# Attention, two feed-forward layers, one core: a written order for the first 22 blocks

## The chip, the cores and the metric

The kernel runs on one core of a Trainium2 chip. The metric is the device time of one execution in microseconds, as the median of several executions. TensorE (PE) does the matmuls and loads their weights (PEld), VectorE (DVE), ScalarE (ACT) and GpSimd (POOL) do the elementwise work, and SyncE (SP) issues nearly all DMAs. Each engine carries out its own instructions strictly in the order in which they were written; an instruction whose input or buffer isn't ready holds up everything behind it on that engine.

## The reference, cut to what matters

```
a = exp(phi - max over sequence); a = a / (sum + 1e-9)      # phi: 8 x 8 x 576 x 32
k_m, v_m = a^T k, a^T v                                     # 32 memory rows per head
p = softmax(q k_m^T / 8);  attn = p v_m                     # q, k, v: 8 x 8 x 576 x 64
x = attn as 4608 x 512
h = x @ w_in;  g = h - tanh(h);  x = g @ w_out              # 512 -> 2048 -> 512
h = x @ w_in2; g = h if h > 0 else exp(h) - 1; out = g @ w_out2
```

The weights arrive as 64-bit floats and are turned into 32-bit ones on the chip.

## The kernel before, in words

**Attention units.** There are 16 units u0 to u15, one per batch and group of four heads. A unit is a Python generator (`Attention.unit`) that writes its instructions in some twenty steps: column maxima of phi (`cmax`, DVE), their transpose (`mT`, PE), the maximum (`nmax`, DVE), a diagonal (`dmax`), its broadcast (`bmax`, PE; copied by ACT into `bm`), `a = phi - bm`, the exponential (ACT), the memory matmuls (`km`, PE), normalisation (`rs`, `kvs`), transposes of q (`pq`, PE; `qT`, ACT) and of the memory (`kT_ps`), scores (`sc`, PE), a transpose into `s` (DVE), softmax on `s` (L237 to L245), a transpose into `phl`, a split into high and low part (ACT, then L255), and a store to DRAM.

**Conversions.** A generator `conv` loads 512 KB of raw weights, takes the magnitude on ACT into the one PSUM buffer `cv_m` (L55), works on it in two pairs of DVE instructions (L57 and L58, L61 and L64) and, for w_out, splits it (ACT L69, POOL L71). There are three raw buffers. Twelve conversions have to be over before block 2.

**First layer.** A half-block is one quarter of the columns of w_in for 288 tokens: `h_unit` (12 matmuls of 128x288 per row below, L374), then the activation on `h_ps` in pieces: ACT `t` (tanh, L385), `u` (L386), `s` (L387) and `big` (L396); POOL `v` (L392); DVE L401, L406 and L410; then the split `g` (ACT L416, POOL L417). Two x units (12 matmuls each, `x_ps`, L432) multiply the g of earlier half-blocks by w_out. `vw_unit` (L356, L360, L361) multiplies the attention's v_m into w_in; a half-block can't begin before its vw is there. I count half-blocks from 0; two make a block, and there are 64 blocks.

**What sets the order.** The string `PLAN` names for each half-block the pieces in their order: H the h unit, A the three ACT pieces, B, R, d, e, p the other pieces, G the split of the half-block before, X an x unit, V the vw unit. U or u moves every live attention unit on by one step, C or c the conversions. So units and conversions advance by rounds, all together. The PSUM pool `misc` has three banks, which bmax, km, pq, sc, vw_ps and x_ps share.

**Second layer.** `step2` writes for unit idx the h unit, the activation's first part (`e_a`), the split of the unit before (`e_c`: ACT L517, POOL L518), the activation's second part (`e_b`) and the output matmuls of unit idx-2 (L534). The last two units of all have nothing behind them. `store` puts each result of 128 rows into DRAM with two DMAs, all on SP's queue.

Of the kernel before, what the change touches and what calls it, by code (L numbers as in the profile page):

```python
# [26 lines left out]
TB = 256  # L27
# [8 lines left out]
PLAN = ((1, "WHCABLlXRUGVXdepcCcu"),  # L36
        (14, "WHABLlXRCUGVXdepcCcu"),
        (44, "lWHLABCXRUXGdeVucp", "WcHAlBUXLRCVGdecXup"),
        (64, "WHAVUBCRlGdULYXUUecp", "WLHuARlCBXVduueYGp"),
        (128, "WuHALRlBCuVXedGYcpU", "lWHuABXRUdCLuYVuUeGp", "WlHUABYRLCdueXucVGp", "UWHLAVRlCUdXBeXGp"))  # L40
# [6 lines left out]
def convert(nc, pool, psum, raw, dst, whole=False):  # L47
# [7 lines left out]
    nc.scalar.activation(m, w_hi.bitcast(F32), ACTF.Abs)  # L55
    yield
    nc.vector.tensor_scalar(m, m, hi_lim, lo_lim, op0=ALU.min, op1=ALU.max)  # L57
    nc.vector.tensor_scalar(mu, mu, 3, 0x3FFFFFFF, op0=ALU.logical_shift_left, op1=ALU.bitwise_and)  # L58
    yield
    a = pool.tile(list(w_hi.shape), F32, tag="a", name="cv_a")  # L60
# [19 lines left out]
class Attention:  # L80
# [46 lines left out]
    def unit(self, u, nxt, eng, first_p=None):  # L127

        nc, wk, sm = self.nc, self.wk, self.sm
        b, g = divmod(u, 2)  # L130
# [26 lines left out]
        (nc.vector if u < 6 else eng).tensor_scalar(dmax, ident, nmax, None, op0=ALU.mult)  # L157
# [10 lines left out]
        eng.tensor_tensor(av, ph, bm.rearrange("p h (o m) -> p h o m", o=1).to_broadcast([96, 4, 6, M]),  # L168
                          op=ALU.subtract)
        yield  # L170
        if eng is nc.gpsimd:
            yield
# [21 lines left out]
        nc.vector.tensor_scalar(kvs, twice, rs, None, op0=ALU.mult)  # L194
# [43 lines left out]
        nc.vector.tensor_tensor(s, s, smax.to_broadcast([128, 18, M]), op=ALU.subtract)  # L238
# [6 lines left out]
        eng.tensor_tensor(s, s, smax.to_broadcast([128, 18, M]), op=ALU.mult)  # L245
# [7 lines left out]
        for t, src in parts:  # L253
            nc.scalar.activation(t[:, 0], src, ACTF.Copy)
            eng.tensor_tensor(t[:, 1], src, r32(t[:, 0]), op=ALU.subtract)  # L255
# [12 lines left out]
def make_const(nc, const):  # L268
# [7 lines left out]
    return {"ident": ident, "ones": ones, "bias": bias}  # L276

# [42 lines left out]
class Moe1:  # L320


    def __init__(self, tc, ctx, const, p_dram, x2_dram):
# [8 lines left out]
        self.vw, self.p, self.g, self.x2, self.work, self.x2_pool = {}, {}, {}, {}, {}, {}  # L332
# [46 lines left out]
    def g_a(self, n, pg):  # L379

        nc, w, bias = self.nc, self.work[n, pg], self.const["bias"]
# [4 lines left out]
        nc.scalar.activation(u, w[0], ACTF.Square)  # L386
        nc.scalar.activation(s, u, ACTF.Square, bias=bias[:, 0:1], scale=G_S)  # L387
# [24 lines left out]
    def g_d(self, n, pg):  # L412
        nc = self.nc
        s = self.work.pop((n, pg))[3]
        g = self.g_p.tile([128, 2, 2, NB], F32R, tag="g", name="g")
        nc.scalar.activation(g[:, 0], s, ACTF.Copy)  # L416
        nc.gpsimd.tensor_tensor(g[:, 1], s, r32(g[:, 0]), op=ALU.subtract)  # L417
        self.g[n, pg] = g
# [31 lines left out]
class Moe2:  # L450
# [70 lines left out]
    def o_unit(self, u):  # L521
# [6 lines left out]
        for tg in range(n_t):  # L528
# [8 lines left out]
            if k == last:  # L537
# [5 lines left out]
                self.store(c * TB + 128 * tg, o)  # L543

    def store(self, t0, o):
        done = 0
        while done < 128:
# [5 lines left out]
            self.nc.sync.dma_start(out=rows[p:p + step], in_=o[done:done + step])  # L553
# [3 lines left out]
def moe_kernel(tc, q, k, v, phi, w1, w2, w3, w4, out):  # L557
    nc = tc.nc
    with ExitStack() as top, tc.manual_schedule():
# [26 lines left out]
        def need(kind, pg, with_units=False):  # L586
            while not all((1, kind, pg, c) in converted for c in range(2)):
                cv.round()
                if with_units:
                    units.round()  # L590

        def conv(layer, kind, pg, c, lead=2):
# [6 lines left out]
            else:  # L599
                r0 = 256 * pg + 128 * c  # L600
                nc.sync.dma_start(out=raw, in_=w[r0:r0 + 128, :])
            for k in range(lead + 1):
# [20 lines left out]
            yield from convert(nc, cv_p, cv_ps, raw, dst, whole)  # L623
# [16 lines left out]
        for what in "phi", "kv", "q0", "q1":  # L640
            at0.load(0, what)
            at1.load(1, what)
        at1.load(2, "phi")
# [287 lines left out]
```

## Time and profile before

| what | value |
|---|---|
| median of 3 runs | 1657.15 us (1656.73 to 1658.26) |
| the profiled execution | 1656.48 us, of which the span from first to last instruction is 1654.7 us |
| PE busy | 1580.8 us, 96% of the span |
| DVE, ACT, POOL busy | 1143.8, 906.7, 744.6 us |
| mean granted TensorE clock | 0.982 of full speed |
| first h unit begins | 63.20 us |

A row of a view names the start in us, the duration in us, the engine, the line and the instruction with the tile that it writes and those that it reads. The bracket at its end is the idle time of that engine just before, and what ended it.

### The profile page before, as it was taken

What the parts mean: (1) busy time and instruction counts of PE and PEld (TensorE: products, weight loads), DVE (VectorE), ACT (ScalarE), POOL (GpSimd) and SP (SyncE); (2) the same over time, 40 slices, a digit from 0 to 9 for tenths busy, and PEclk for the clock granted to TensorE, in tenths of its full rate; (3) what the DMA queues carried; (4) which work ended last, traced back from release to release, by engine and by line L of the source; (5) the groups of instructions that cost most, each with busy time, mean ns of one, the idle gap of its engine ahead of it and who ended that gap; (6) DMA issues with size and microseconds to landing.
All of it is one profiled execution on the core that took longest, in us unless ns stands there. A gap on an engine that the chain in (4) does not pass through costs nothing.

```text
span 1654.7 us, 28097 instructions
## 1 busy us (share of the span) xinstructions
PE 1580.8 (96%) x10742; PEld 1380.2 (83%) x10742; DVE 1143.8 (69%) x1664; ACT 906.7 (55%) x1639; POOL 744.6 (45%) x526
## 2 busy tenths in 40 slices
PE   5679989899999999999999999999999999999998
PEld 4558878788999999999999888888888888888886
DVE  5777768889998888887656655656565556555644
ACT  2356778678888888888753333333333333333332
POOL 0235667676765577777643332323222323232322
PEclk9779999999999999999999999999999999999999
DMA  9656677677754577675695211212121212121100
GB/s 238 184 170 185 188 210 217 197 226 237 249 182 153 180 222 223 220 223 179 204 336 217 91 64 39 89 39 89 39 77 40 75 39 76 41 74 52 38 1 26
DMA packets 142213, 232.89 MB, mean 141 GB/s; under 512 B 8704, under 2 KB 102912, under 8 KB 140032
## 3 DMA queue, kind: packets, MB, share of 16 engines
q1 hardware_dynamic: 142080, 231.11, 44.8%
q8 instruction: 84, 1.38, 0.3%
q14 instruction: 49, 0.40, 0.1%
HBM read 157.68 MB, written 73.40 MB: 140 GB/s over the span
## 4 chain that ended last, share of the span: by engine, by line
PE 81%; DVE 6%; ACT 4%; issue 4%; POOL 3%; DMA 1%; SPq 0%; POOLq 0%; ACTq 0%; DVEq 0%
PE h_ps L492 24%; PE o_ps L534 24%; PE x_ps L432 19%; PE h_ps L374 10%; PE vw_ps L356 2%; PE km L180 1%; DVE s L406 1%; POOL v L392 1%; DMA q<-in_q_dram 1%; POOL g L417 1%; ACT t L385 1%; ACT u L386 1%; DMA raw<-in_moe_w_in_dram 1%; DVE h_ps L401 0%; ACT x L438 0%
## 5 line engine op out<-in xcount | busy, mean ns | idle before, releaser
L518 POOL TENSOR_TENSOR e<-hm,e 128x512 fp32r<-128x512 f32 x144 | 186.6, 1296 | 573.7 <-ACT e L517 526.3
L432 PE MATMUL x_ps<-g,w 128*128 128x288 f32 x3072 | 437.5, 297 | 5.9 <-ACT x L438 2.2
L432 PEld LDWEIGHTS x_ps<-g,w 128*128 128x128 f32 x3072 | 417.4, 189 | 11.6 <-ACT x L438 3.1
L492 PE MATMUL h_ps<-x,wi 128*128 128x512 f32 (+1 forms) x1920 | 422.2, 370 | 0.0
L534 PE MATMUL o_ps<-wo,e 128*128 128x512 f32 x1728 | 420.4, 392 | 0.7 <-POOL e L518 0.7
L492 PEld LDWEIGHTS h_ps<-x,wi 128*128 128x128 f32 x1920 | 336.0, 188 | 65.7
L534 PEld LDWEIGHTS o_ps<-wo,e 128*128 128x128 f32 x1728 | 323.6, 188 | 72.4 <-POOL e L518 1.1
L503 ACT ACTIVATE t_ps<-hm 128x512 f32<-128x512 f32 x144 | 86.7, 602 | 501.5 <-DVE hm L502 501.5
L417 POOL TENSOR_TENSOR g<-s,g 128x576 fp32r<-128x576 f32 x128 | 198.2, 1549 | 115.4 <-ACT g L416 91.5
L392 POOL TENSOR_TENSOR v<-t,u 128x576 f32<-128x576 f32 x128 | 185.3, 1448 | 129.5 <-ACT u L386 105.8
L509 DVE SCALAR_TENSOR_TENSOR hm<-hm,t_ps 128x512 f32<-128x512 f32 x144 | 99.0, 687 | 200.3 <-ACT hm L504 200.3
L374 PE MATMUL h_ps<-p,vw 128*128 128x288 f32 x1536 | 235.5, 303 | 0.0
L374 PEld LDWEIGHTS h_ps<-p,vw 128*128 128x128 f32 x1536 | 214.4, 192 | 13.2 <-issue 11.7
L502 DVE TENSOR_SCALAR hm<-h_ps 128x512 f32<-128x512 f32 x144 | 99.5, 691 | 126.7 <-PE h_ps L492 124.0
L406 DVE SCALAR_TENSOR_TENSOR s<-s,v 128x576 f32<-128x576 f32 x128 | 137.2, 1072 | 54.3 <-ACT big L396 35.7
L385 ACT ACTIVATE t<-h_ps 128x576 f32<-128x576 f32 x128 | 83.4, 652 | 100.9 <-issue 42.6
L410 DVE COPY_PREDICATED s<-big,h_ps 128x576 f32<-128x576 uint32 x128 | 105.9, 828 | 7.9
L401 DVE TENSOR_TENSOR h_ps<-h_ps,t 128x576 f32<-128x576 f32 x128 | 97.1, 759 | 18.9 <-ACT u L386 18.5
L387 ACT ACTIVATE s<-u,bias 128x576 f32<-128x576 f32 x128 | 99.6, 778 | 16.3 <-POOL g L417 6.0
L510 DVE SCALAR_TENSOR_TENSOR hm<-hm,t_ps 128x512 f32<-128x512 f32 x144 | 98.9, 687 | 5.0
L511 DVE TENSOR_TENSOR hm<-hm,h_ps 128x512 f32<-128x512 f32 x144 | 98.9, 687 | 5.0
L504 ACT ACTIVATE hm<-hm 128x512 f32<-128x512 f32 x144 | 91.0, 632 | 13.1
(88 smaller groups left out, 1553.5 us busy)
## 6 DMA issues: line engine op xcount, KB each, us to landing
x_dram<-x SPq DMA_DIRECT2D x128, 288.0 KB, 3.4
xr<-x_dram SPq DMA_DIRECT2D x72, 512.0 KB, 3.8
p<-p_dram SPq DMA_DIRECT2D x62, 576.0 KB, 5.4
raw<-in_moe_w_in_dram SPq DMA_DIRECT2D x32, 512.0 KB, 4.5
raw<-in_moe_w_out_dram SPq DMA_DIRECT2D x32, 512.0 KB, 4.5
w_dram<-wst SPq DMA_DIRECT2D x32, 512.0 KB, 3.9
kv<-in_k_dram SPq DMA_DIRECT2D x16, 576.0 KB, 6.1
kv<-in_v_dram SPq DMA_DIRECT2D x16, 576.0 KB, 7.9
```

Source lines behind the costliest of these rows:

```text
L374: nc.tensor.matmul(ps[:, j, :NB], lhsT=vw[a][:, kc, c0 + 128 * j:c0 + 128 * j + 128], rhs=p[:, kc, b, :], start=(k == 0), stop=(k == 5))
L385: nc.scalar.activation(t, w[0], ACTF.Tanh)
L387: nc.scalar.activation(s, u, ACTF.Square, bias=bias[:, 0:1], scale=G_S)
L392: nc.gpsimd.tensor_tensor(v, t, u, op=ALU.mult)
L406: nc.vector.scalar_tensor_tensor(s, s, G_B, v, op0=ALU.add, op1=ALU.mult)
L410: self.nc.vector.copy_predicated(s, big.bitcast(U32), d)
L417: nc.gpsimd.tensor_tensor(g[:, 1], s, r32(g[:, 0]), op=ALU.subtract)
L432: nc.tensor.matmul(ps, lhsT=wo[pg][a][:, j, 128 * dm:128 * dm + 128], rhs=self.g[n, pg][:, b, j, :], start=(k == 0), stop=(k == 11))
L492: nc.tensor.matmul(out, lhsT=w3[:, a, kc, 128 * j:128 * j + 128], rhs=x[:, b, kc, :], start=(i == 0), stop=(i == 11))
L502: nc.vector.tensor_scalar(hm, w[0], 0.0, None, op0=ALU.min)
L518: nc.gpsimd.tensor_tensor(e[:, 1], hm, r32(e[:, 0]), op=ALU.subtract)
L534: nc.tensor.matmul(acc, lhsT=e[:, a, jj, 128 * tg:128 * tg + 128], rhs=w4[:, b, j, :], start=(k == 0 and jj == 0 and i == 0), stop=(k == l ...
```

## The change

The order of the first 22 blocks (44 half-blocks) is no longer made by rounds. `BEGIN` lists the steps before the first half-block, `SCRIPT` those of each of the first 44: u3 moves unit 3 on by one step, c6 conversion number 6, v writes a vw unit, p0 loads unit 0's phi. The three ACT pieces of A are now A, a and s, and the low part of the split (POOL) is g. From half-block 44 on the old plan goes on, with a, s and g right behind A and G.

`POOLS` says per unit which of the steps d (`dmax`), a, m (the softmax's product), l (the low part) run on POOL and whether k (`kvs`) runs on ACT; before, u0 and u1 had all on DVE, u2 to u5 a, m and l on POOL, and the others all four on POOL. In effect m of u3 and of u9 and l of u10 go from POOL to DVE, and `kvs` of u0 and u8 from DVE to ACT.

In the second layer the split of the last but one unit is written ahead of the last h unit, and half of the last eight stores go on ACT's queue.

```diff
-PLAN = ((1, "WHCABLlXRUGVXdepcCcu"),
...
+SCRIPT = ("W H c5 l c6 c6 A a R s B X u2 u3 u4 u4 G g V X d e L c6 c8 c7 u2 p c5 u3",
+          "W H c7 A a s L B l X R u2 c6 c6 u3 u4 G g X V d e p c7 c7 c9 c8 u2",
...
+POOLS = ("k", "", "aml", "al", "aml", "aml", "daml", "daml", "damlk", "dal", "dam", "daml", "daml", "daml", "daml", "daml")
+CLAMPS = ()
...
-        eng.tensor_tensor(s, s, smax.to_broadcast([128, 18, M]), op=ALU.mult)
+        on("m").tensor_tensor(s, s, smax.to_broadcast([128, 18, M]), op=ALU.mult)
...
+        if "k" in where:
+            nc.scalar.activation(kvs, twice, ACTF.Copy, scale=rs)
+        else:
+            nc.vector.tensor_scalar(kvs, twice, rs, None, op0=ALU.mult)
...
         def step2(idx):
+            if idx == len(seq) - 1:
+                m2.e_c(seq[idx - 1])
             if idx < len(seq):
                 m2.h_unit(seq[idx])
                 m2.e_a(seq[idx])
-            if 1 <= idx <= len(seq):
+            if 1 <= idx <= len(seq) and idx != len(seq) - 1:
                 m2.e_c(seq[idx - 1])
...
-                self.store(c * TB + 128 * tg, o)
-
-    def store(self, t0, o):
+                end = wide and c + 2 == NT // TB
+                self.store(c * TB + 128 * tg, o, (nc.scalar if tg % 2 == 0 else nc.sync) if end else nc.sync)
...
+    def step(self):
+        if not self.over:
+            try:
+                next(self)
+            except StopIteration:
+                pass
```

The first place is DVE shortly before the first half-block; `vw` is the split of the vw unit's result, `p` that of the first units' softmax, `cv_m` and `cv_a` belong to conversions. Before:

```order
L255 TENSOR_TENSOR p<-phl,p 128x288 x2
L57 TENSOR_SCALAR cv_m<-cv_m 128x512
L58 TENSOR_SCALAR cv_m<-cv_m 128x512
L61 SCALAR_TENSOR_TENSOR cv_m<-raw,cv_m 128x512
L64 SCALAR_TENSOR_TENSOR cv_a<-raw,cv_m 128x512
L361 TENSOR_TENSOR vw<-vw_ps,vw 128x256 x4
```

And now, from the same p on:

```order
L311 TENSOR_TENSOR p<-phl,p 128x288 x2
L439 TENSOR_TENSOR vw<-vw_ps,vw 128x256 x2
L107 TENSOR_SCALAR cv_m<-cv_m 128x512
L110 TENSOR_SCALAR cv_m<-cv_m 128x512
L113 SCALAR_TENSOR_TENSOR cv_m<-raw,cv_m 128x512
L116 SCALAR_TENSOR_TENSOR cv_a<-raw,cv_m 128x512
L439 TENSOR_TENSOR vw<-vw_ps,vw 128x256 x2
```

The first of the two vw splits has moved ahead of a whole conversion.

The second place is PE from half-block 1's h unit to half-block 2's; `sc` are unit u2's scores, `bmax` the broadcast of unit u3's or u4's maxima. Before:

```order
L374 MATMUL h_ps<-p,vw 128x288 x12
L77 MATMUL sc<-ident 128x128 x5
L230 MATMUL sc<-qT,kT 32x288 x8
L206 MATMUL pq<-ident,q 128x96 x3
L160 MATMUL bmax<-dmax,ones 96x128
L374 MATMUL h_ps<-p,vw 128x288 x12
```

And now:

```order
L452 MATMUL h_ps<-p,vw 128x288 x12
L129 MATMUL sc<-ident 128x128 x5
L286 MATMUL sc<-qT,kT 32x288 x8
L452 MATMUL h_ps<-p,vw 128x288 x12
L213 MATMUL bmax<-dmax,ones 96x128
L262 MATMUL pq<-ident,q 128x96 x6
```

The h unit has moved ahead of the bmax and of the transposes of q.

The third place is POOL in half-blocks 28 and 29; `w` is a conversion's split, `s` the softmax's product. Before:

```order
L392 TENSOR_TENSOR v<-t,u 128x576
L71 TENSOR_TENSOR w_3263<-cv_a,w_3262 128x512
L245 TENSOR_TENSOR s<-s,smax 128x576
L157 TENSOR_SCALAR dmax<-ident,nmax 128x128
L417 TENSOR_TENSOR g<-s,g 128x576
L392 TENSOR_TENSOR v<-t,u 128x576
L255 TENSOR_TENSOR phl<-phl 128x2x288
L168 TENSOR_TENSOR a<-phi,bm 96x4x6x32
```

And now:

```order
L476 TENSOR_TENSOR v<-t,u 128x576
L123 TENSOR_TENSOR w_3296<-cv_a,w_3295 128x512
L210 TENSOR_SCALAR dmax<-ident,nmax 128x128
L505 TENSOR_TENSOR g<-s,g 128x576
L476 TENSOR_TENSOR v<-t,u 128x576
L221 TENSOR_TENSOR a<-phi,bm 96x4x6x32
```

The product s has gone from in front of dmax, and the low part phl from in front of a.

## Rows read from the trace of the kernel before

**Rows 1.** Windows of the span: busy us (instructions) per engine, PE clock, DMA share.

```profile
0.00:64.00 64.00, 37.37 (x332) 28.11 (x333) 42.57 (x80) 18.29 (x43) 6.95 (x11) 0.84 0.91 232
64.00:116.00 52.00, 35.98 (x302) 27.09 (x300) 34.79 (x61) 25.81 (x53) 19.64 (x14) 0.71 0.56 160
116.00:437.00 321.00, 296.37 (x2903) 265.00 (x2903) 264.88 (x400) 241.63 (x476) 212.04 (x151) 0.99 0.69 207
437.00:841.00 404.00, 404.00 (x3481) 390.76 (x3480) 334.76 (x479) 338.12 (x591) 276.31 (x188) 1.00 0.63 205
```

**Rows 2.** Timeline of PE, 58 to 116 us: start, duration, instruction, idle before.

```profile
59.03 1.10 PE L356 MATMUL vw_ps<-w,vm 64*32 64x256 f32 x14 [7.21 <-DVE vw L361]
...
63.20 1.84 PE L374 MATMUL h_ps<-p,vw 128*128 128x288 f32 x12
...
80.72 0.74 PE L160 MATMUL bmax<-dmax,ones 128*96 128x128 f32 x2 [4.08 <-DVE s L234]
...
113.49 1.02 PE L356 MATMUL vw_ps<-w,vm 64*32 64x256 f32 x8 [3.33 <-DVE w L64]
```

**Rows 3.** Timeline of DVE, 54 to 112 us.

```profile
55.02 0.83 DVE L255 TENSOR_TENSOR p<-phl,p 128x288 fp32r<-128x288 f32 x2 [1.05 <-ACT p L254]
55.77 0.69 DVE L57 TENSOR_SCALAR cv_m<-cv_m 128x512 f32<-128x512 f32 x1
...
58.56 0.75 DVE L361 TENSOR_TENSOR vw<-vw_ps,vw 128x256 fp32r<-128x256 f32 x2
...
90.28 0.70 DVE L57 TENSOR_SCALAR cv_m<-cv_m 128x512 f32<-128x512 f32 x1 [5.11 <-ACT cv_m L55]
...
108.82 0.70 DVE L57 TENSOR_SCALAR cv_m<-cv_m 128x512 f32<-128x512 f32 x1 [1.04 <-ACT cv_m L55]
...
110.94 1.18 DVE L238 TENSOR_TENSOR s<-s,smax 128x576 f32<-128x576 f32 x1
```

**Rows 4.** Timeline of ACT, 84 to 90 us.

```profile
84.44 0.65 ACT L385 ACTIVATE t<-h_ps 128x576 f32<-128x576 f32 x1 [3.17 <-PE h_ps L374]
...
89.64 0.61 ACT L55 ACTIVATE cv_m<-raw 128x512 f32<-128x512 f32 x1
```

**Rows 5.** Timeline of PE, 209 to 327 us.

```profile
209.91 0.46 PE L160 MATMUL bmax<-dmax,ones 128*96 128x128 f32 x2 [1.36 <-POOL dmax L157]
...
232.19 0.46 PE L160 MATMUL bmax<-dmax,ones 128*96 128x128 f32 x2 [1.34 <-POOL dmax L157]
...
304.36 0.46 PE L160 MATMUL bmax<-dmax,ones 128*96 128x128 f32 x2 [3.40 <-POOL dmax L157]
304.58 3.07 PE L374 MATMUL h_ps<-p,vw 128*128 128x288 f32 x12
...
318.14 2.16 PE L180 MATMUL km<-kv,a 96*32 96x192 f32 x48 [1.38 <-ACT a L173]
...
326.08 1.16 PE L356 MATMUL vw_ps<-w,vm 64*32 64x256 f32 x32 [1.60 <-DVE kvs L194]
```

**Rows 6.** Timeline of POOL, 302 to 312 us.

```profile
302.07 1.16 POOL L245 TENSOR_TENSOR s<-s,smax 128x576 f32<-128x576 f32 x1 [0.41 <-DVE smax L244]
303.20 1.11 POOL L157 TENSOR_SCALAR dmax<-ident,nmax 128x128 f32<-128x128 f32 x1
...
310.45 1.43 POOL L255 TENSOR_TENSOR phl<-phl 128x576 fp32r<-128x576 f32 x1
```

**Rows 7.** Timeline of DVE, 315 to 326 us.

```profile
315.98 2.83 DVE L238 TENSOR_TENSOR s<-s,smax 128x576 f32<-128x576 f32 x1
...
323.13 0.73 DVE L242 TENSOR_REDUCE smax<-s 128x18 f32<-128x576 f32 x1
...
325.44 0.48 DVE L194 TENSOR_SCALAR kvs<-km,rs 128x256 f32<-128x256 f32 x1
```

**Rows 8.** Timeline of the end: PE's last matmuls.

```profile
1643.46 5.33 PE L534 MATMUL o_ps<-wo,e 128*128 128x512 f32 x22 [0.68 <-POOL e L518]
```

**Rows 9.** Timeline of the end: DVE's last copy.

```profile
1648.83 0.69 DVE L542 COPY o<-o_ps 128x512 f32<-128x512 f32 x1 [0.69 <-PE o_ps L534]
```

**Rows 10.** Timeline of the end: SP's DMA issues.

```profile
1647.38 4.06 SPq L553 DMA_DIRECT2D out_dram<-o  x8
```

More of the change, by code (lines that the diff above doesn't have):

```diff
@@ L584, in moe_kernel, with need, conv @@
         converted = set()
[L586 to L592, printed above, removed]
+        def need(kind, pg):
+            for c in range(2):
+                while (1, kind, pg, c) not in converted:
+                    if (kind, pg, c) in named:
+                        named[kind, pg, c].step()
+                    else:
+                        cv.round()
+        def conv(layer, kind, pg, c):
             w = {("i", 1): w1, ("o", 1): w2, ("i", 2): w3, ("o", 2): w4}[kind, layer]
@@ L657, in moe_kernel, with all_units @@
         first_p = [m1.new_p(0, n) for n in range(2)]
-        units = Staged()
-        for u in range(2 * B):
-            units.at((0, 1, 7, 13, 19, 25, 32, 39, 45, 52, 58, 65, 78, 85, 92, 99)[u], unit(u))
-        while 1 not in p_done:
-            if units.rounds >= 7:
-                cv.half()
-            units.round()
-            if units.rounds >= 7:
-                cv.round()
+        units = [Work(unit(u)) for u in range(2 * B)]
+        vw0 = []
+        def all_units():
+            live = [g for g in units if g.begun and not g.over] or [g for g in units if not g.begun][:1]
+            for g in live:
+                g.step()
@@ new lines, in first_vw, with side @@
+        def first_vw():
+            if not vw0:
+                m1.new_vw(0, 0, 0)
+            if len(vw0) < 2 and all((1, "i", len(vw0), c) in converted for c in range(2)) and vm_done >= {0, 1}:
+                m1.vw_unit(vm[:, 0], {len(vw0): wi[len(vw0)][0]}, 0, [len(vw0)])
+                vw0.append(True)
+        def side(step):
+            if step[0] == "u":
+                units[int(step[1:])].step()
+            elif step[0] == "c":
+                convs[int(step[1:])].step()
+            elif step == "v":
+                first_vw()
+            else:
+                u, what = int(step[-1]), {"p": "phi", "k": "kv", "q": "q0", "r": "q1"}[step[0]]
+                (at1 if u else at0).load(u, what)
@@ L667, in moe_kernel @@
+        for step in BEGIN.split():
+            side(step)
+        while 1 not in p_done:
+            all_units()
         pro.close()
@@ L824, in moe_kernel @@
                 pg = 2 * sw + i
[L825 to L826 removed]
+                hb = 2 * bi + i
+                for step in SCRIPT[hb].split() if hb < len(SCRIPT) else next(p[hb % len(p)] for end, *p in PLAN if hb < end):
+                    if len(step) > 1:
+                        side(step)
+                    elif step == "W":
                         if vw_next and bi > 1 and i == 1 and not at1.held:
```

130 lines of the change are left out of this document (79 added, 51 removed), and 44 rows, old and new, of the table SCRIPT.

## The prediction

> **What bounds the kernel now.** I read the windows first. From 437 to 841 us PE is busy 404.00 of 404.00 us at full clock; in the three stretches ahead of it PE is busy 37.37 of 64, 35.98 of 52 (at a granted clock of 0.71) and 296.37 of 321 us [rows 1]. So the whole kernel is PE's work, and what can be won in the first 22 blocks is PE's idle time there: 64 + 52 + 321 - 369.72 = 67.3 us. Since nothing waits behind 437 us until the very end, a microsecond saved before it stays saved.
>
> Then I read the timeline of PE for its long waits. Before the first half-block PE waits 7.21 us for the split of the vw unit on DVE, then 4.08 us with bmax, which needs a bank that DVE's transposes (L234) still hold, and 3.33 us for the twelfth conversion [rows 2]. Later there are five of 1.3 to 3.4 us [rows 5]. In each the awaited engine did not have too much work; it did something else first. That is what a different order can mend.
>
> The timeline of DVE shows the other side. It is busy 34.79 of 52 us in the second stretch and 264.88 of 321 in the third [rows 1], and in the second its longest gap is 5.11 us, before conversion 10, until ACT has taken the magnitude [rows 3]. ACT does that at 89.64, behind the whole activation of half-block 2, whose tanh had itself waited 3.17 us for PE's h unit [rows 4]. And that h unit stood on PE behind the bmax with its 4.08 us. So this is one chain: bank, bmax, h unit, tanh, magnitude, conversion, vw.
>
> **The sum, stage by stage.** *Up to the first h unit (term A).* The h unit needs two vw units; the second needs banks which the first frees when DVE splits it. Before, DVE did a whole conversion from 55.77 to the split at 58.56 [rows 3]; now that conversion stands behind the split (first place in the order). That is 2.8 us. DVE's wait of 1.05 us for ACT's high part of p [rows 3] falls away too, since ACT now has that high part ahead of a conversion's magnitude. A = 3.9. Below, the split could be held up on ACT instead: 0. Above, the whole wait: 7.2.
>
> *Half-blocks 0 to 3 (term B).* PE's second place: the h unit of half-block 2 no longer stands behind the bmax, and the 4.08 us go. I take 4.08 and not DVE's 5.11, since it is the cause of that gap. The twelfth conversion waited 1.04 us for its magnitude and then had a subtraction of 1.18 us between its halves [rows 3]; the new list puts two magnitudes in a row on ACT, and the subtraction behind the conversion. B = 4.1 + 1.0 + 1.2 = 6.3. Behind the second magnitude ACT queues a unit's split and the tanh of half-block 3, which would wait for DVE to finish conversion 11; PE then waits with them, so B's low end is 0. Its high end takes in the 3.33 us: 9.6.
>
> *Half-blocks 4 to 43 (term C).* Five waits of PE [rows 5] meet a changed order. The bmax at 209.91 now comes behind the next h unit, which covers its 1.36 us. At 232.19 the product s (1.16 us on POOL) no longer stands ahead of dmax: 1.2. At 304.36 the same, third place in the order: dmax starts 1.13 us earlier, from 303.20 to 302.07 [rows 6]; and the h unit behind this wait took 3.07 us against 1.84 for the same twelve matmuls at 63.20 [rows 2, 5], which a shorter wait may give back: 1.1 + 1.2 = 2.3. At 318.14 the a that km waits for stood on POOL behind phl, of 1.43 us [rows 6]: 1.4. At 326.08 kvs on DVE stood behind the reductions that begin at 323.13 [rows 7], now a half-block earlier: 1.6. Together 7.9. Against it stand the three instructions that go from POOL to DVE. The trace has no such product on DVE in this stage; the nearest row is a subtraction of the same size, 1.18 us at 110.94 [rows 3], or 2.83 at 315.98, where POOL worked beside it [rows 7]. I take 1.18, the one nearest to an undisturbed time, so 3.5 us, and let all of it count, as DVE is 83% busy there. The two kvs that leave DVE (0.48 each [rows 7]) lie as long on ACT, which is less loaded; I take nothing, with 0.5 each way. C = 7.9 - 3.5 = 4.4. Its ends: 7.9 if the three are hidden, and 7.9 - 8.5 = -0.6 at 2.83 each.
>
> *The rest of the first 22 blocks.* Some thirty more steps move by one to three places. No wait of PE over 1.3 us ends at them, so I set them to nothing; the cover is PE's own x units, two of which lie in each half-block. Without the cover each would cost a wait like those of [rows 5].
>
> *The end (term D).* PE waits 0.68 us for the last but one unit's split on POOL [rows 8]. That split now comes before the last h unit; 0.7 gained. Then eight issues take SP from 1647.38 to 1651.44 [rows 10], 0.51 each, and the last copy is over at 1649.52 [rows 9]; so 1.92 us of issuing follow it. With two queues only its own two issues do, 1.0: gain 0.9. Issuing on ACT isn't in the trace; I price it as on SP. D = 1.6, and 0.7 if the transfers themselves fill that time.
>
> Sum: 3.9 + 6.3 + 4.4 + 1.6 = 16.2. The profiled execution took 1656.48 us in all, 1.8 more than its span, and lies 0.67 under the median of the runs shown. 1656.48 - 16.2 + 0.67 = **1641.0 us**.
>
> **The rivals.** *Score banks (slower).* In half-blocks 9, 12, 15, 25, 28, 35 and 42 the scores of a unit now stand ahead of at least one x unit that they used to follow. Two of three banks are then full until DVE has transposed them, and an x unit must wait. For it: the 4.08 us of [rows 2] are just such a wait. Against it: in the new order DVE's transposes come ahead of that half-block's activation, so DVE should be there first. Price: 7 x 4.08 = 28.6, so 1641.0 + 28.6 = 1669.6. It decides from 16.2 / 7 = 2.3 us per place on.
>
> *Two engines at one port.* The product of 2.83 us at 315.98 [rows 7] ran beside POOL's work; if all three moved instructions meet that, C is -0.6 instead of 4.4, and the time 1646.0. The Trainium skill says in "SBUF — State Buffer", section "Who interferes with whom", that a VectorE instruction with two SBUF inputs and a GpSimd instruction that reads SBUF exclude each other for the whole of the first; the row agrees that such an instruction can be long, and by that rule POOL would be held up as well.
>
> *The weights' loads.* If the conversions of half-blocks 0 to 3 come earlier but their raw data doesn't, B falls away: 1647.3. For it: only three raw buffers. Against it: the DMA share is 0.56 in that stretch [rows 1], and DVE's gaps there end at ACT, not at a load [rows 3].
>
> *All waits go.* A 7.2, B 9.6, C 7.9, D 1.6: 26.3, so 1630.9. For it: the granted clock of 0.71 from 64 to 116 [rows 1], which fewer gaps may raise.
>
> *No change.* The list could be the old order written out: 1657.2. The three places in the order speak against it, and so does the full PE from 437 on.
>
> **How the numbers follow.** The forecast 0.48, the port 0.12, the loads 0.14, all waits gone 0.12, no change 0.05, score banks 0.09. The range from 1630 to 1652 holds the first three and, with 1630.9 near its edge, half of the fourth: 0.80; it takes in A and B at their low ends one at a time (1644.9 and 1647.3). A measurement of this kernel tells about 0.2%, 3.3 us, from no change: faster 0.86, within that 0.05, slower 0.09.
>
> **What would show it.** The first h unit starts near 59 us instead of 63.2; half-block 4's near 105 instead of 115; PE is full from about 422 instead of 437; the bmax waits of [rows 5] are under 0.5 us; the last store is issued within 1.2 us of the last copy. Waits of x_ps for s (L234's new line) over 2 us in half-blocks 9 to 42 would prove the slower rival; ACT idle ahead of the second magnitude in half-block 2 with PE waiting for tanh's followers would break B.

## The result, and the profile after

The changed kernel took 1638.89 us as the median of 4 runs (1636.32 to 1642.95), against 1657.7 for the kernel before in as many runs beside it: a ratio of 0.9887, with an interval of 0.9863 to 0.991. The forecast was 1641.0, so the kernel is faster, as foreseen, and by 18.8 us where 16.2 were summed. The profiled execution took 1638.01 us with a span of 1635.9.

The windows of the span after, with the columns and stretches of [rows 1]:

```profile
0.00:64.00 64.00, 42.73 (x359) 32.15 (x363) 44.37 (x82) 22.37 (x50) 9.51 (x13) 0.81 0.90 240
64.00:116.00 52.00, 40.13 (x384) 31.56 (x384) 44.60 (x76) 29.84 (x60) 21.62 (x17) 0.80 0.66 174
116.00:437.00 321.00, 301.80 (x2953) 270.97 (x2952) 272.50 (x408) 249.27 (x487) 217.62 (x154) 0.99 0.72 220
437.00:841.00 404.00, 404.00 (x3463) 391.46 (x3463) 325.31 (x466) 331.08 (x582) 266.66 (x182) 1.00 0.64 208
```

PE does more in the same time in the first three stretches, and from 437 on it is full as before. DVE's share in the second rose from 34.79 to 44.60 us of 52, at a DMA share that rose from 0.56 to 0.66: the same work, closer together.

Since PE is full later on, the starts of the h units tell where the time came from. Read from the timeline of PE of both kernels, the difference is what had been gained by then:

| h unit of half-block | before | after | gained |
|---|---|---|---|
| 0 | 63.20 | 58.31 | 4.89 |
| 4 | 114.89 | 103.29 | 11.60 |
| 8 | 155.23 | 143.84 | 11.39 |
| 26 | 282.00 | 268.70 | 13.30 |
| 32 | 329.05 | 309.34 | 19.71 |
| 38 | 370.59 | 350.06 | 20.53 |
| 39 | 379.07 | 360.95 | 18.12 |
| 48 | 435.61 | 417.88 | 17.73 |
| end of the span | 1654.7 | 1635.9 | 18.8 |

The timeline of PE after, at the places of [rows 2]:

```profile
53.70 1.10 PE L434 MATMUL vw_ps<-w,vm 64*32 64x256 f32 x14 [0.61 <-DVE vw L439]
...
58.31 1.84 PE L452 MATMUL h_ps<-p,vw 128*128 128x288 f32 x12
...
69.57 1.88 PE L452 MATMUL h_ps<-p,vw 128*128 128x288 f32 x12
71.29 0.38 PE L213 MATMUL bmax<-dmax,ones 128*96 128x128 f32 x2
74.15 0.83 PE L262 MATMUL pq<-ident,q 96*128 96x96 f32 x6 [2.47 <-DVE s L290]
```

The wait of 7.21 us ahead of the first half-block has shrunk to 0.61. The bmax doesn't wait at all. But its bank wait isn't gone; 2.47 us of it stand at the next `pq`, *behind* the h unit of half-block 2 and no longer ahead of it, so that ACT and DVE have that unit's activation to do meanwhile.

The places of [rows 5], in the same timeline:

```profile
288.85 0.46 PE L213 MATMUL bmax<-dmax,ones 128*96 128x128 f32 x2 [0.45 <-POOL dmax L210]
...
300.25 2.16 PE L233 MATMUL km<-kv,a 96*32 96x192 f32 x48 [1.43 <-ACT a L226]
...
305.83 1.09 PE L434 MATMUL vw_ps<-w,vm 64*32 64x256 f32 x32
```

Of 3.40 us for dmax 0.45 are left, of the 1.60 for kvs nothing; km still waits its 1.43. One long wait is new, at half-block 38; in the timeline of all engines there:

```profile
342.84 1.84 POOL L221 TENSOR_TENSOR a<-phi,bm 96x768 f32<-96x768 f32 x1 [0.49 <-ACT bm L219]
343.66 2.44 DVE L299 TENSOR_SCALAR smax<-smax 128x18 f32<-128x18 f32 x1
344.64 1.42 POOL L505 TENSOR_TENSOR g<-s,g 128x576 fp32r<-128x576 f32 x1
...
355.92 0.48 DVE L250 TENSOR_SCALAR kvs<-km,rs 128x256 f32<-128x256 f32 x1
356.55 1.70 PE L520 MATMUL x_ps<-g,w 128*128 128x288 f32 x11 [2.55 <-DVE kvs L250]
```

An x unit waits 2.55 us for kvs. And 12 us ahead of it DVE spent 2.44 us on an addition to 18 columns, which ended 0.04 us after POOL's second product did. That row is the key to half of the experiments below.

The end, as in [rows 9, 10]:

```profile
1630.06 2.16 SPq L642 DMA_DIRECT2D out_dram<-o  x4
...
1630.72 0.69 DVE L630 COPY o<-o_ps 128x512 f32<-128x512 f32 x1 [0.68 <-PE o_ps L622]
1630.88 1.18 ACTq L642 DMA_DIRECT2D out_dram<-o  x2
```

The last store is issued 0.81 us after the last copy (1632.22 against 1631.41), where it was 1.92.

### The profile page after: what moved, and what is told of

It is laid out like the page before. It is cut to its first block, busy times and chain, and to the rows that moved or that the text cites. A ratio compares the mean times of both kernels' runs of the same rounds, so it can differ in the third digit from the quotient of the medians.

```text
span 1635.9 us, 28086 instructions
## 1 busy us (share of the span) xinstructions
PE 1577.9 (96%) x10742; PEld 1377.7 (84%) x10742; DVE 1146.1 (70%) x1666; ACT 907.8 (55%) x1640; POOL 740.8 (45%) x523
## 4 chain that ended last, share of the span: by engine, by line
PE 83%; DVE 6%; ACT 4%; POOL 4%; issue 3%; DMA 0%; POOLq 0%; ACTq 0%; DVEq 0%
PE h_ps L580 24%; PE o_ps L622 24%; PE x_ps L520 20%; PE h_ps L452 10%; PE vw_ps L434 2%; PE km L233 1%; POOL g L505 1%; POOL v L476 1%; DVE s L490 1%; ACT t L463 1%; DVE cmax L193 0%; ACT s L471 0%; ACT u L467 0%; DVE cv_m L113 0%; DVE cv_m L107 0%
## 5 line engine op out<-in xcount | busy, mean ns | idle before, releaser
L490 DVE SCALAR_TENSOR_TENSOR s<-s,v 128x576 f32<-128x576 f32 x128 | 134.8, 1053 | 49.0 <-ACT big L480 35.8
L480 ACT ACTIVATE big<-u,bias 128x576 f32<-128x576 f32 x128 | 97.9, 765 | 0.9 <-DVE s L494 0.8
```

The lines of the kernel that those rows point to most:

```text
L490: nc.vector.scalar_tensor_tensor(s, s, G_B, v, op0=ALU.add, op1=ALU.mult)
```

## The experiments

Each kernel is the changed one with the edit shown. Between two timed medians of this kernel some 3 us are noise, so I read each edit's effect from the h unit starts of its profile, and give the time beside it.

One execution of each kernel was traced, and PE's granted clock isn't the same in all of them. Kernels with the changed kernel's order up to the first half-block begin it at 57.23 to 58.94 us. Half-block 5 takes 8.1 to 8.5 us where the clock stays at 1.00, and 9.4 to 9.6, as in the changed kernel, where it is 0.84 to 0.86 in the mean. In half-block 38 eight kernels have the same wait of 2.54 to 2.56 us; it takes 10.9 us in two of them (the changed kernel and the first of experiment 2), where the clock stays at 1.00, and 12.0 to 12.3 in the other six, where it falls (0.86 in the mean). So one or two us ahead of half-block 6, and 1.2 at half-block 38, needn't be the edit's.

**1. Term A: the first vw unit late.** Both vw units are written at the end of the list, as the rounds had it.

```diff
-"... u0 u1 u3 v c5 u2 c7 c4 u3 c4 u2 c5 v"
+"... u0 u1 u3 c5 u2 c7 c4 u3 c4 u2 c5 v v"
```

> The changed kernel with both first vw units written at the end of the opening list, so that on VectorE a conversion stands again between the high part of p and the first vw split. Theory (term A: the second vw unit waits for banks that the first split frees): the second vw unit waits 5 to 7 us again, the first h unit starts at 61 to 62.5 us instead of 58.3, and since nothing behind absorbs it the total is 2.8 to 4 us longer than the changed kernel's 1638.9. Rival (the half-blocks 0 to 43 have their own pace, set by conversions and units on VectorE, and absorb it): the first h unit moves the same way, but half-block 44 starts less than 1 us later and the total stays within 1 us.

Measured: 1647.12 us, ratio 0.9937 (0.9923 to 0.9951). A long wait is back in the timeline of PE, though with 4.08 us a shorter one than the 5 to 7 expected:

```profile
56.19 1.10 PE L434 MATMUL vw_ps<-w,vm 64*32 64x256 f32 x14 [4.08 <-DVE vw L439]
```

The first h unit is 2.77 us late, which is what the prediction set down for the conversion ahead of the split (2.8). Up to half-block 6 the lateness falls to 1.31 (half-block 5 has the full clock here); by half-block 8 it is 4.52 and from 39 on 5.7, above the 2.8 to 4 expected. The 3.2 us in half-blocks 6 and 7 are not the vw unit's; experiment 5 names them. The last 1.2 are the clock in half-block 38:

```profile
361.12 2.25 PE L520 MATMUL x_ps<-g,w 128*128 128x288 f32 x12 [2.56 <-DVE kvs L250]
```

**2. Term B: bmax, and what takes the third bank.** First bmax alone goes ahead of the h unit of half-block 2, as before:

```diff
-"W H A a X s u4 R u3 B u2 L l u4 c8 c10 ..."
+"W u4 H A a X s R u3 B u2 L l u4 c8 c10 ..."
```

> The changed kernel with one step of unit u4 ahead of half-block 2's h unit, so that only TensorE's order differs: the bmax stands ahead of that h unit again. Theory (term B: bank, bmax, h unit, tanh, magnitude, conversion, vw are one chain): TensorE waits about 4 us at this bmax, VectorE waits 4 to 5 us for the magnitude of conversion 10, half-block 4 starts 4 us later, total 4 us longer than the changed kernel. Rival (VectorE's conversions would come no earlier anyway): the h unit of half-block 2 moves by 4 us, half-block 4 by less than 1 us, total within 1 us.

Measured: 1638.83 us, ratio 0.9897 (0.9881 to 0.9912). Every half-block starts 0.3 to 0.6 us later and that is all; bmax, ahead of the h unit, waits for nothing. So the order of bmax and h unit, to which the prediction gave the 4.08 us, isn't their cause by itself. In the kernel before a transpose of q (`pq`) stood ahead of both. Two score tiles and that one hold all three banks. The second kernel puts both there:

```diff
-"W H A a X s u4 R u3 B u2 L l u4 c8 c10 ..."
+"W u3 u4 H A a X s R B u2 L l u4 c8 c10 ..."
```

> Only the third half-block's list is changed: the two steps that issue the transposes of q (u3) and the next of unit 4 stand ahead of its h unit, as they did before, and bmax ahead of the h unit too. If banks are the cause (two score tiles and one tile of q hold all three, and bmax waits until VectorE has copied the scores out), a wait of 2 to 4 us is back on TensorE in front of this h unit, it starts at 93 to 95 us in place of 91.15, and the conversions behind it are later by the same, so that half-block 8 starts at 145 to 147 in place of 143.84 and the kernel takes 1640 to 1643 us. Rival: the conversions alone set the pace here and do not see these banks: the h unit is later but half-block 8 within 0.5 us of 143.84, and the time within 1 us of 1638.9.

Measured: 1642.89 us, ratio 0.9915 (0.9898 to 0.9932). In the timeline of PE:

```profile
70.19 0.47 PE L262 MATMUL pq<-ident,q 96*128 96x96 f32 x3
74.74 0.46 PE L213 MATMUL bmax<-dmax,ones 128*96 128x128 f32 x2 [4.08 <-DVE s L290]
74.95 2.69 PE L452 MATMUL h_ps<-p,vw 128*128 128x288 f32 x12
```

It is the wait of the kernel before, to the digit. The h unit is 5.38 us late, half-block 4 4.39, and all to half-block 38 4.1 to 4.3 (5.5 from 39 on, with the clock). Half-block 8, at 148.03, is later than the 145 to 147 expected; the 91.15 of the expectation is the start of half-block 3, which begins at 93.78. So the price was right in size, and a bank held by `pq` is the cause of the wait. The rival in this expectation, that the conversions set the pace here whatever PE does, falls.

**3. Term C: the table of engines.** First the whole old table, then the product of unit 3 alone, on POOL again:

```diff
-POOLS = ("k", "", "aml", "al", "aml", "aml", "daml", "daml", "damlk", "dal", "dam", "daml", ...)
+POOLS = ("", "", "aml", "aml", "aml", "aml", "daml", "daml", "daml", "daml", "daml", "daml", ...)
```

> The changed kernel with the table of engines as before: the product of u3 and u9 and the low part of u10 on GpSimd, the two kvs on VectorE; the order of all else is the new one. Theory by my sum (each moved instruction costs VectorE 1.2 us that TensorE waits for): 2 to 3.5 us faster than the changed kernel. Rival (GpSimd was the engine that others waited for at these places, and VectorE had room): 1 to 4 us slower.

Measured: 1643.84 us, ratio 0.9914 (0.9897 to 0.993). It is slower and not 2 to 3.5 us faster, as the rival had it. Half-block 6 begins 0.80 us *earlier* than in the changed kernel, half-block 8 4.09 later.

```diff
-POOLS = ("k", "", "aml", "al", ...
+POOLS = ("k", "", "aml", "aml", ...
```

> Only one letter of the table: the last product with the reciprocal sums of unit 3 runs on GpSimd again. If this one instruction is what the whole old table cost up to half-block 8 (it stood ahead of GpSimd's low parts of the last conversions there), half-block 8 starts near 148 us in place of 143.84, and the time is 1642 to 1645 us. Rival: the old table's loss comes from the other two units as well or instead: half-block 8 within 1 us of 143.84, and the time within 1.5 us of 1638.9.

Measured: 1639.41 us, ratio 0.9895 (0.9871 to 0.992). No loss at half-block 8 (3.08 us early, 1.77 of which it already had at half-block 3, ahead of the moved product). So my reading of the first of the two, that POOL's product was the cost, was wrong for the traced execution; its rival, the other two units, is what is left until experiment 5. The other 1.1 us of the 3.08 are half-block 5 at full clock, so the product itself is worth nothing that can be seen. The six times lie in two groups, 1635.2 to 1636.1 and 1642.7 to 1646.5, and the trace is of the first: whether the cost comes back in the second isn't shown.

**4. Term D: the end as before.** The split and the stores of the second layer are put back.

```diff
-            if idx == len(seq) - 1:
-                m2.e_c(seq[idx - 1])
...
-                self.store(c * TB + 128 * tg, o, (nc.scalar if tg % 2 == 0 else nc.sync) if end else nc.sync)
+                self.store(c * TB + 128 * tg, o, nc.sync)
```

> The changed kernel with the second layer's end as before: the last but one unit's split behind the last h unit, all last stores on SyncE's queue. Theory (term D, with what the two profiles showed): TensorE waits 0.7 us for that split again, eight issues follow each other on one queue, total 1.0 to 1.6 us longer than the changed kernel. Rival (the transfers themselves fill the end): within 0.4 us.

Measured: 1638.49 us, ratio 0.9891 (0.9874 to 0.9908). By half-block 100 its profile is 0.88 us behind the changed kernel's (1.2 of it from the clock in half-block 38), its span is 1.6 longer; so 0.7 us belong to the end. The time can't tell that. But the profile showed something else: half-block 6 was 3.52 us early, and half-block 8 only 0.30.

**5. The collision in half-blocks 6 and 7.** Three small moves were meant to make a better kernel: one magnitude earlier on ACT, one later, and a conversion pair on DVE behind kvs in half-block 38.

```diff
-"... V X d e p c10 c10 u3 c11 u5",
+"... V c10 X d e p c10 u3 u5",
...
-"u2 W H A a s u4 B L l c10 ..."
+"u2 W H A a c11 s u4 B L l c10 ..."
...
-"l W H L A a s B c24 c25 c27 X R u12 u13 u14 u15 X ..."
+"l W H L A a s B c24 c27 X R u12 u13 u14 u15 c25 X ..."
```

> Three moves in the list and nothing else. The magnitude of conversion 11 goes ahead of a copy-out of x on ScalarE (VectorE waited 1.81 us for it at 92.36); the magnitude of the next conversion goes behind the first two gelu steps of half-block 3 (it held ScalarE for 3.79 us, and with it the copy-outs that TensorE waits 2.26 us for at 100.30); in half-block 38 one conversion pair on VectorE goes behind kvs (1.4 of the 2.55 us that TensorE waits for kvs). If the conversions set the pace up to half-block 8, what is won on them is won there: half-block 8 starts 1.5 to 3 us earlier than 143.84, another 1.2 to 1.4 us come at half-block 38, and the time is 1634.5 to 1636.5 us. Rival: the conversions wait next for the loads of their raw words or for GpSimd: half-block 8 within 0.5 us of 143.84, only the wait for kvs shrinks, and the time is 1637 to 1639 us.

Measured: 1640.53 us, ratio 0.99 (0.9883 to 0.9918), no gain. It was 2.96 us early at half-block 6 and 3.05 late at half-block 8. The timeline of all engines between:

```profile
126.02 1.83 POOL L221 TENSOR_TENSOR a<-phi,bm 96x768 f32<-96x768 f32 x1 [2.16 <-ACT bm L219]
126.45 3.40 DVE L490 SCALAR_TENSOR_TENSOR s<-s,v 128x576 f32<-128x576 f32 x1
127.80 1.43 POOL L505 TENSOR_TENSOR g<-s,g 128x576 fp32r<-128x576 f32 x1
...
133.87 0.74 PE L262 MATMUL pq<-ident,q 96*128 96x96 f32 x3 [2.54 <-DVE vw L439]
134.46 8.83 PE L129 MATMUL x_ps<-ident 128*128 128x128 f32 x52
```

And at the same place in the changed kernel:

```profile
127.50 0.75 DVE L490 SCALAR_TENSOR_TENSOR s<-s,v 128x576 f32<-128x576 f32 x1
...
128.84 1.82 POOL L221 TENSOR_TENSOR a<-phi,bm 96x768 f32<-96x768 f32 x1 [1.74 <-ACT bm L219]
...
130.63 1.42 POOL L505 TENSOR_TENSOR g<-s,g 128x576 fp32r<-128x576 f32 x1
...
134.24 6.00 PE L129 MATMUL x_ps<-ident 128*128 128x128 f32 x52
```

The DVE step of the gelu (L490) takes 0.75 us when it is over before POOL's two products begin. When it starts 0.4 us after the first of them, it is held until the second is over at 129.23, and ends 0.62 us later. The conversion, the reductions and the split of vw stand behind it on DVE; PE waits 2.54 us for vw, and the 52 filler matmuls ahead of the x unit (on the identity, their result isn't used), 6.00 us in the changed kernel, take 8.83. The windows of the kernel with three moves show why:

```profile
125.00:135.00 10.00, 7.05 (x68) 5.32 (x67) 9.69 (x13) 7.50 (x16) 4.87 (x4) 0.92 0.50 162
135.00:145.00 10.00, 10.00 (x70) 9.80 (x72) 5.39 (x8) 1.89 (x5) 6.45 (x5) 0.74 0.64 206
```

After the idle time PE's granted clock falls to its lower level (0.50 of full, 1.2 GHz) for a part of the second window, to 0.74 in the mean. In the changed kernel it is 1.00 there.

All kernels of this study can be sorted by that one row. The time from the h unit of half-block 6 to that of half-block 8:

| L490 beside POOL's a and g | kernels | half-block 6 to 8, us |
|---|---|---|
| clear of them: 0.74 to 0.76 us (before: 1.35) | before; changed; both of experiment 2; unit 3's product alone; and below both with the swap, the one without the additions, the second of experiment 7 | 21.4 to 22.1 |
| held: 3.37 to 3.39 us; fillers 6.07 | experiments 1 and 4; below the first of experiment 7 | 24.7 to 24.9 |
| held: 3.38 and 3.40 us; fillers 7.70 and 8.83 | old table; three moves | 26.5 and 27.7 |

To test whether it is the cause, DVE's two gelu steps of half-block 6 were written ahead of a conversion pair, which touches no other engine's order; first with the three moves, then with the old table:

```diff
-"W H A a s B X L l R u3 c14 u4 u5 u6 G g V d X c15 e p ..."
+"W H A a s B X L l R u3 d e c14 u4 u5 u6 G g V X c15 p ..."
```

> The three moves of the run before, and on VectorE alone in half-block 6 the two gelu steps (h_ps times t's difference, then s<-s,v) ahead of one conversion pair in place of behind it. Theory: in the run with three moves s<-s,v began at 126.45, just after GpSimd had begun two products back to back (126.02 to 129.23), and was held until both were over (3.40 us in place of 0.75); TensorE then waited 2.54 us for vw at 133.87, its granted clock fell to 0.50, and the 52 filler matmuls took 8.83 us in place of 6.00. With the swap s<-s,v runs from about 125.1 to 125.9, before GpSimd's pair: it takes 0.75, the wait for vw is under 0.5, the fillers take 6.0, half-block 8 starts at 140.5 to 141.5 (146.89 in the run with three moves, 143.84 in the changed kernel), and the time is 1634 to 1637 us. Rival: the three moves starve TensorE at this place in any case: the wait and the low clock come back with the swap too, half-block 8 at 145 or later, and the time 1639 us or more.

Measured: 1637.63 us, ratio 0.9888 (0.9871 to 0.9904). L490 takes 0.76 us, the long wait for vw is gone, the fillers take 6.00, and half-block 6 to 8 21.59 us: the mechanism came out as expected. The start didn't: half-block 8 at 143.25 and not 141. The three moves, of which I had expected 1.5 to 3 us, are worth some 0.5 at half-block 6. The 2.96 us that their first profile had was mostly the clock: 1.3 came in half-block 5, which had a granted clock of 1.00 then, 0.85 in the changed kernel and 0.84 with the swap, and 2.0 in half-block 2, where the kernel with the swap gained nothing. Both kernels have the same order up to there, and in the window from 80 to 90 us the one (first row) was granted 0.72, the other 0.50:

```profile
80.00:90.00 10.00, 7.86 (x82) 4.97 (x83) 8.70 (x16) 3.74 (x11) 4.28 (x4) 0.72 0.94 264
```

```profile
80.00:90.00 10.00, 7.99 (x74) 4.72 (x74) 8.69 (x16) 3.02 (x8) 3.56 (x3) 0.50 0.97 289
```

The third move did what it was to do: the wait for kvs fell from 2.55 to 1.21 us in both.

> The changed kernel with the old table of engines, and the same swap on VectorE in half-block 6. With the old table alone s<-s,v took 3.38 us at 128.62 beside the same two GpSimd products (128.18 to 131.38), TensorE waited 2.54 us for vw at 136.03 and the fillers took 7.70 us. If this one collision is the old table's loss up to half-block 8, the swap gives all of it back: half-block 8 at 142.5 to 143.5 in place of 147.93, and the time is 1638 to 1640.5 us (1643.84 with the old table alone). Rival: GpSimd's own longer queue is the loss (its low parts of the last conversions are late): half-block 8 stays above 146 and the time above 1642 us.

Measured: 1641.88 us, ratio 0.9908 (0.9891 to 0.9924). Half-block 8 begins at 143.38, within the expected bounds, 4.55 us earlier than with the old table alone. So that collision was the old table's loss up to there, and POOL's longer queue wasn't. The time is still above what I had expected, as the timeline shows a second collision:

```profile
156.79 1.85 POOL L221 TENSOR_TENSOR a<-phi,bm 96x768 f32<-96x768 f32 x1
...
157.46 3.96 DVE L299 TENSOR_SCALAR smax<-smax 128x18 f32<-128x18 f32 x1
158.60 1.40 POOL L476 TENSOR_TENSOR v<-t,u 128x576 f32<-128x576 f32 x1
159.96 1.42 POOL L505 TENSOR_TENSOR g<-s,g 128x576 fp32r<-128x576 f32 x1
...
166.69 2.60 PE L233 MATMUL km<-kv,a 96*32 96x192 f32 x48 [1.64 <-DVE vw L439]
```

From half-block 8 to 12 it takes 3.0 us longer than the changed kernel. But that isn't the price of the collision alone. The kernel with three moves and the one with the swap on top of them have the same one (L299 takes 3.96 and 3.97 us), and the same wait of PE behind it; with the swap, at a granted clock of 1.00, 1.45 us are lost there, without it, at 0.89, 4.57. With the swap, and then without it:

```profile
166.57 2.16 PE L233 MATMUL km<-kv,a 96*32 96x192 f32 x48 [1.64 <-DVE vw L439]
```

```profile
170.20 3.35 PE L233 MATMUL km<-kv,a 96*32 96x192 f32 x48 [1.63 <-DVE vw L439]
```

**6. Without the small instruction.** Both additions of 1e-9 are left out; in float32 they change no bit of sums that are at least 1.

```diff
-        nc.vector.tensor_scalar(smax, smax, GUARD, None, op0=ALU.add)
...
-        nc.vector.tensor_scalar(rs, km[:, 2 * D:2 * D + 1], GUARD, None, op0=ALU.add)
-        nc.vector.reciprocal(rs, rs)
+        nc.vector.reciprocal(rs, km[:, 2 * D:2 * D + 1])
```

> The addition of 1e-9 to the sums of both softmaxes is left out (one small VectorE instruction in each place; sums are at least 1 in float32, so it changes no bit of them). If the small instruction itself is what GpSimd stretches (0.17 us alone, 0.93 us in the mean over 14, 2.44 at 343.66), VectorE wins up to 13 us of busy time between 64 and 440, the 2.55 us wait for kvs at 356.55 shrinks by 2, and the time is 1635.5 to 1637.5 us. Rival: GpSimd holds back whatever VectorE instruction comes next, so the stretch moves to the reciprocal or the transpose behind it: VectorE's busy time falls by less than 3 us, and the time stays within 1 us of 1638.9.

Measured: 1635.66 us, ratio 0.9878 (0.9856 to 0.9899), and 3.5 us ahead in the profile from half-block 39 on (1.1 of them from half-block 5, at full clock here, and 1.5 from half-block 38, where the wait for kvs is 1.44). The groups of DVE from 64 to 440 us in the changed kernel, then here (busy us, mean ns of one):

```profile
L490 DVE SCALAR_TENSOR_TENSOR s<-s,v 128x576 f32<-128x576 f32 x52 | 60.5, 1163 | 10.0 <-POOL v L476 9.6 <-ACT big L480 0.4
L299 DVE TENSOR_SCALAR smax<-smax 128x18 f32<-128x18 f32 x14 | 13.0, 928 | 0.5
...
L298 DVE TENSOR_REDUCE smax<-s 128x18 f32<-128x576 f32 x14 | 10.4, 744 | 0.7 <-ACT s L296 0.7
L300 DVE RECIPROCAL smax<-smax 128x18 f32<-128x18 f32 x14 | 3.7, 267 | 0.5
```

```profile
L490 DVE SCALAR_TENSOR_TENSOR s<-s,v 128x576 f32<-128x576 f32 x52 | 63.9, 1229 | 12.1 <-POOL v L476 9.9 <-ACT big L480 1.8
...
L300 DVE RECIPROCAL smax<-smax 128x18 f32<-128x18 f32 x14 | 3.7, 267 | 0.5
```

The 13.0 us are gone, 3.4 of them come back on L490, and the reciprocal behind is not held at all (267 ns in both). So not whatever comes next is held; some instructions are, and the reduction and the reciprocal never (725 to 758 ns and 266 to 270 ns over all copies of all kernels after the change).

The Trainium skill says in "SBUF — State Buffer", section "Who interferes with whom", that a VectorE instruction with two SBUF inputs contends with a GpSimd instruction that reads SBUF, that one in a two-port mode, which a tensor_scalar can enter, and GpSimd block each other in full, and that a reduction on trn2 never contends. The rows of L490 and of the reductions agree; that the addition ran in such a mode they don't show, only that it is held as this rule has it.

They show one thing more: whether VectorE gets its turn between two GpSimd instructions that follow one another directly isn't settled by the rule. In the five collisions of half-block 6 it didn't, nor did the addition at 343.66. In the changed kernel L490 began beside the first of two such instructions 13 times from 64 to 440 us, and each time it did: it ended 0.6 us after the first, and the second took some 0.5 us longer than its like elsewhere. One of them, in half-block 7:

```profile
136.61 1.30 POOL L123 TENSOR_TENSOR w<-cv_a,w 128x512 fp32r<-128x512 f32 x1
137.32 1.20 DVE L490 SCALAR_TENSOR_TENSOR s<-s,v 128x576 f32<-128x576 f32 x1
137.84 1.95 POOL L311 TENSOR_TENSOR phl<-phl 128x576 fp32r<-128x576 f32 x1
```

What decides between the two isn't shown.

**7. Put together.** First without the additions, with unit 3's product on POOL, and the conversion pair behind kvs; then with the two magnitudes and the swap of experiment 5 as well.

> The changed kernel without the additions of 1e-9 (they change no bit of sums of at least 1), with unit 3's product on GpSimd again, and in half-block 38 the conversion pair on VectorE behind kvs. If the three add up: 3.5 from the first and 1.9 from the second as measured at half-block 48, and 1 to 1.4 for the wait for kvs: 1632 to 1634 us. Rival: the same instructions at other times meet other products on GpSimd, and a new collision takes back 2 to 4 us: 1635 to 1638 us.

Measured: 1636.02 us, ratio 0.9865 (0.9846 to 0.9884). The rival came true in the traced execution: L490 took 3.37 us at 127.60, beside the same two products, and half-block 6 to 8 24.66. Two of the five executions took 1631.9 us, the other three 1636.0 to 1636.8; whether the two were clear of the collision isn't shown. The 1.9 us that the expectation takes from unit 3's product were the clock of that profile (experiment 3).

> All of these together: the additions left out, unit 3's product on GpSimd, the two moved magnitudes, the conversion pair behind kvs, and the swap in half-block 6. If all gains add up (3 us from the magnitudes by half-block 6 beside those of the run before), 1629.5 to 1632 us. Rival: conversions are no longer the pace once two of these are in, or a collision elsewhere takes them back: no better than the version without the moved magnitudes, 1632 to 1636 us.

Measured: 1633.19 us, ratio 0.9858 (0.9842 to 0.9874), with a span of 1628.8: the fastest of all, though above the 1629.5 to 1632 expected and within the rival's bounds. L490 is clear of POOL's pair, and the wait for kvs is gone. Its windows:

```profile
64.00:116.00 52.00, 38.66 (x403) 29.54 (x396) 46.29 (x80) 32.52 (x65) 26.03 (x20) 0.90 0.71 190
116.00:437.00 321.00, 306.41 (x2983) 276.61 (x2983) 267.31 (x386) 252.71 (x493) 218.90 (x155) 1.00 0.73 222
```

In the long stretch DVE is busy 267.31 us in place of 272.50, and PE 306.41 in place of 301.80. Against the changed kernel it is 7.1 us in the profile (some 2 of them with the clock of the stretch ahead, 0.90 for 0.80) and 5.7 in the medians; the intervals of the two ratios still overlap.

## Why the prediction was right, and where not

**The whole.** That PE is the bound, and that what is won ahead of 437 us stays, held: the gain at half-block 48 is 17.73 us, and the end adds 1.07. That PE's waits there are all there is to win didn't quite: its clock gave a part. The signs came out: the first h unit at 58.3 (59 forecast), half-block 4 at 103.3 (105), PE's last wait ahead of the full stretch at 412 (422), the three bmax waits at 0.45 or less, the last store 0.81 after the last copy.

That the sum came so near is in part luck. In each of three stretches PE carries out the same number of instructions before and after, so its time can be parted into waiting and work (us):

| stretch | forecast | gained | less waiting | less work | granted clock |
|---|---|---|---|---|---|
| start to half-block 0 (A) | 3.9 | 4.9 | 7.0 | -2.1 | 0.84, then 0.80 |
| half-block 0 to 4 (B) | 6.3 | 6.7 | 3.3 | 3.4 | 0.72, then 0.80 |
| half-block 4 to 48 (C) | 4.4 | 6.1 | 4.7 | 1.5 | 0.99, then 0.99 |

The second row comes from these windows, before and after:

```profile
63.20:114.89 51.69, 35.67 (x304) 26.78 (x303) 34.55 (x58) 24.70 (x50) 19.64 (x14) 0.72 0.55 160
```

```profile
58.31:103.29 44.98, 32.24 (x305) 24.09 (x303) 36.72 (x63) 24.77 (x50) 18.95 (x14) 0.80 0.74 199
```

The sum priced waits, and the clock only with the 1.2 us of one h unit in C. Of the waits, A gave 3.1 us more than forecast and B 3.0 less; the clock made good what B lacked. The clock differs between traced executions too: in the same stretch it was 0.85 for unit 3's product alone, which has the changed kernel's order of PE, and the stretch took 43.91 us in place of 44.98.

**Term A, 3.9 forecast, 4.9 measured.** The 2.8 us for the conversion ahead of the split came back as 2.77 when that alone was undone. The other 2.1, where I had 1.1 for the high part of p, weren't tried alone. Kernels with this order differ by up to 1.7 us there, so that the first is so near is chance and the second may be. The wait that was to shrink by 3.9 went from 7.21 to 0.61; a lower clock took back 2.1.

**Term B, 6.3 forecast, 6.7 measured (half-block 0 to 4).** The step that failed is "the h unit of half-block 2 no longer stands behind the bmax, and the 4.08 us go": bmax may stand ahead, if `pq` doesn't, 2.47 us of wait stand at the next `pq` now, and PE waits 3.3 us less in all, not 6.3. The other half of the gain is PE's clock. With the banks full the stretch takes 3.8 us longer, of which 1.9 are waits and 1.9 work at a lower clock (34.14 us for 32.24, at 0.78 for 0.80); so the 4.1 to 4.4 us that the order costs up to half-block 38 equal the price of 4.08 partly by chance. The other 2.2 of the sum weren't taken apart.

**Term C, 4.4 forecast, 6.1 measured (half-block 4 to 48).** The five waits were priced at 7.9: of these 2.6 up to half-block 26, where 1.7 to 1.9 were gained, and 5.3 behind it, where half-blocks 26 to 32 gained 6.4 (4.4 of it waits). Two steps failed. One is the 1.4 us for km, "the a that km waits for stood on POOL behind phl": phl no longer stands ahead, and km still waits 1.43. The wait ends at ACT's exponential, which ACT took 3.1 us after POOL's subtraction was over before (317.26 against 314.20) and 3.7 after it now (299.37 against 295.71).

The other is the one subtracted: 3.5 us for three instructions moved to DVE, "let all of it count, as DVE is 83% busy". They do take 3.2 us on DVE (products of 0.76 and 1.70 us, one subtraction of 0.74), but unit 3's product back on POOL changed neither half-block 6 to 8 (21.40 us, 21.65) nor the time. For the other two there is only the old table with the swap: half-blocks 12 to 26 took 0.3 us less with it, 26 to 32 1.3 more. What took time in its place I hadn't in the sum: the wait of 2.55 us for kvs in half-block 38, behind a conversion pair (1.34 of it, by the move in experiment 5) and behind the held addition (1.1, by its removal); with both edits it is gone.

**Term D, 1.6 forecast, 0.7 to 1.1 measured.** Of the split's 0.7 only 0.2 came (the wait is 0.46 where it was 0.68 [rows 8]); with the second queue the last issue follows the last copy by 1.1 us less.

**The rivals.** Score banks: x_ps waits for `s` 0.4 us in all between 58 and 440, so it didn't come; in half-block 2, with a third tile in the third bank, it is real, at 4.1 us. The loads: between 58 and 116 us no wait of 0.5 us or more was for a load, so this one didn't come. All waits go: they didn't, but its reason, the clock, gave half of term B. One port: I had the mechanism mostly at the wrong instructions. Of the moved ones one met it (unit 9's product, 1.70 us where unit 3's took 0.76); two that the change left alone, L490 and the small addition, meet it or not according to where everything around them falls. One meeting costs 3.0 to 3.2 us in half-blocks 6 and 7 while the clock stays at 1.00, and 4.9 and 6.0 with 0.94 and 0.88; in half-blocks 8 to 11 it costs 1.5, or 3.0 and 4.6 with a lower clock. The changed kernel happens to be clear of it in half-block 6.

**A theory of mine that fell.** After the first four runs I held that the conversions set the pace up to half-block 8, since kernels that were early or late at half-block 6 were not so at half-block 8. The collision explains each of these, and nothing is left for which the conversions are needed: the kernel with full banks, 4.29 us late at half-block 6, is 4.19 late at 8.

**What stays open.** Why PE's clock falls after a wait of 2.54 us in half-block 7 of two kernels and not after 2.54, 2.55 and 2.29 us in the three others, and after the same wait in half-block 38 in six of eight; and why the window from 80 to 90 us is granted 0.50 in some profiles and 0.72 to 0.77 in others with the same order there. Also when VectorE is let in between two GpSimd instructions.

## What to carry to other kernels

In a hand-written order for engines with in-order queues, look for what holds the last free bank before you blame the instruction that waits for it. Then look for instructions whose time varies by three or more between equal copies, VectorE against GpSimd above all: an edit that shifts everything by a microsecond can move one into the other (L490 was clear when it began 0.7 us ahead of POOL's product, and held when it began 0.4 behind), and that will look like the edit's own cost. Before you believe such a cost, undo the collision on one engine alone and see whether the cost goes with it. And part what you gained into less waiting and work that ran at another clock before you credit a term of your sum with it.

## What the runs showed of the hardware

An addition to 128x18 values took 0.17 us alone, and 2.44 beside two GpSimd products in a row, 3.96 beside three. A VectorE step on 128x576 from two SBUF tiles took 0.75 us alone and 3.40 beside two; at most other places where two followed directly it was let in after the first, and a second product took 1.95 us for 1.43. Reductions and reciprocals of the same tiles took 744 and 267 ns in the mean throughout. After 2.3 to 2.5 us of idle time the same 52 filler matmuls took 6.07, 7.70 or 8.83 us; after one wait of 2.55 us the half-block took 10.9 us at a granted clock of 1.00 and 12.1 at 0.86.
